# A gated delta recurrence before a mixture of experts: values carried in spare rows of the state

## The chip, the cores and the metric

The kernel runs on one core of a Trainium2 chip. The core has a matrix engine (TensorE, here PE, with its weight loads shown apart), a vector engine (VectorE, DVE), a scalar engine (ScalarE, ACT), GpSimd (POOL) and SyncE (SP), which here does nothing but issue transfers (DMA). Each engine works through its own instructions in order and waits on semaphores. The metric is the time of one execution on the device in microseconds (us); the figure for a kernel is the median of its runs.

## The reference

Two blocks follow each other, all in float32.

The first is a delta-rule recurrence over 4 batches, 8 heads, 768 steps and a head width of 48. Per batch and head a 48x48 state starts at zero:

```
k_n = k / (norm(k) + 1e-6)
for t in range(768):
    y[t]  = q[t] @ state
    v_old = k_n[t] @ state
    state = state + beta[t] * outer(k_n[t], v[t] - v_old)
```

The result, turned to 3072 tokens of width 384, goes into a mixture of experts with 4 groups of 4 experts. Each token takes the best group by `x @ w_group`, then the best expert of that group, and its output is the product of the two softmax weights with `relu(x @ w1) @ w2`, with w1 of 384x1024 and w2 of 1024x384.

## The kernel before

**The recurrence by chunks.** The 768 steps are cut into 24 chunks of 32 (`C`, `NCH`). All four batches lie side by side in the 128 partitions (32 steps each), and the 8 heads are handled as 4 pairs. Inside a chunk the recurrence is a triangular system, which is inverted explicitly. Four chunks (`RG`) form a group, and one call of `inverse(g)` makes the inverses for the whole group on DVE, in some 120 small instructions (L276 to L374). ACT then spreads the result into `mtb` (L385). `inverse` also yields the norms of the keys, `norm[g]`.

**Work per chunk.** `advance(u)` (L407) has four stages, separated by `yield`:

1. `a_ps` holds the norm-scaled values plus key times state. The scaled values `vh` come from `scale(u)` on DVE (L400), and they get into `a_ps` by a product with the identity (L413); 16 small products with the state follow (L419). ACT copies `a_ps`, negated, to `f` (L423). Query times state goes to `o_ps` (L428).
2. `w_ps` is the inverse times `f` (L436), copied to `w` (L439).
3. `s_ps` adds keys times `w` to the state, which lives in PSUM (L446). Two ACT instructions copy it to `s_bd` in SBUF (L452).
4. The masked query-key products `gq` times `w` complete `o_ps` (L460 in the first 14 chunks, L465 in the last ten), and ACT copies it to `x` (L469).

`s_bd` holds, per pair of heads, 48 rows of one head at partitions 0 to 47 and 48 rows of the other at 64 to 111, so that partitions 48 to 63 and 112 to 127 are empty. The keys and queries `kqt` are laid out in the same way, with zeros in these rows.

`gram(u)` makes the products of keys with keys and queries; it runs ten chunks ahead (`LEAD`). `mask(u)` (L261) multiplies `gq` on DVE by a 0/1 mask. It writes each 32-wide product twice, once per parity of the batch, which stage 4 needs where two batches share one product (L460). In the last ten chunks L465 uses one half only.

**What sets the order.** The whole section is scheduled by hand: every engine runs its instructions in the order in which Python emits them. The loop at L693 emits chunk u. The DVE work of `inverse` and of the routing is a set of generators; `work(n)` lets each of them issue instructions up to a share of a time budget, so the budgets of a chunk, `work(10)`, `work(9)`, `work(14)`, `work(12)`, decide where DVE's instructions stand between the rest. At the end of chunk u come `mask(u + 1)`, `scale(u + 2)` and then SP's transfers: `load_kq(u + 12)` (512 KB, L192, up to u = 11), `load_kv(u + 3)` (448 KB, L196; three buffers, `NV`), the store of `x` (L753), and in some chunks a piece of the first expert's weights (L150, L156). `scale(u)` reads the value half of `kv`, stage 3 the key half. Before the loop, `bursts` ties the first loads to ACT instructions between the first grams, and the first group is inverted, after which `mask(0)`, `scale(1)` and `mtb` follow.

`idle_products` (L686) issues products whose result nobody reads, on PE, behind the last chunk and during the sorting of tokens.

**The experts.** Tokens are sorted by expert, gathered, and each of the 16 experts runs on PE: `hidden` (L872), then `second` (L891), which makes the output in three column blocks of 128 and calls `between(j)` after each. For the last expert `turn_out` (L918) turns the three blocks of each of the two token tiles back by PE, multiplies all 384 columns by the gate on DVE (L925), and scatters the rows by an indirect transfer from POOL (L909).

## Time and profile before

| | |
|---|---|
| median of 3 runs | 523.79 us (521.79 to 524.82) |
| profiled execution | 517.99 us, span 516.0 us, granted clock 0.992 |
| PE busy | 472.9 us (92%) |
| DVE busy | 251.0 us (49%) |
| ACT busy | 185.9 us (36%) |
| POOL busy | 194.1 us (38%) |
| identity product, L413 | 48 instructions, 23.4 us busy |
| state products, L419 / L428 | 20.5 / 19.4 us busy |
| state copy on ACT, L452 | 46 instructions, 37.0 us busy |
| mask, L265 / scaling, L400 | 16.1 / 13.7 us busy on DVE |
| loads of k and v, L196 | 24 of 448 KB, 3.8 us from issue to landing (median) |

PE shows two instructions for each float32 product. The recurrence takes the first 244 us or so of the span, the experts the rest. A share of busy time is an average over both: DVE's 49% is nearly full in the first and mostly idle in the second. In a row of the timeline the first number is the start from the beginning of the span, the second the time taken; a bracket tells how long the engine was idle before and what ended it.

### The profile page before, as it was taken

What the parts mean: (1) busy time and instruction counts of PE and PEld (TensorE: products, weight loads), DVE (VectorE), ACT (ScalarE), POOL (GpSimd) and SP (SyncE); (2) the same over time, 40 slices, a digit from 0 to 9 for tenths busy, and PEclk for the clock granted to TensorE, in tenths of its full rate; (3) what the DMA queues carried; (4) which work ended last, traced back from release to release, by engine and by line L of the source; (5) the groups of instructions that cost most, each with busy time, mean ns of one, the idle gap of its engine ahead of it and who ended that gap; (6) DMA issues with size and microseconds to landing.
All of it is one profiled execution on the core that took longest, in us unless ns stands there. A gap on an engine that the chain in (4) does not pass through costs nothing.

```text
span 516.0 us, 18196 instructions
## 1 busy us (share of the span) xinstructions
PE 472.9 (92%) x7832; PEld 437.1 (85%) x7832; DVE 251.0 (49%) x830; ACT 185.9 (36%) x389; POOL 194.1 (38%) x288
## 2 busy tenths in 40 slices
PE   3446999999999999997999999999999999999993
PEld 3335778888888888884999999999999999999992
DVE  2999999999999995435420122012201111011110
ACT  3224767677676776740111211121111111111110
POOL 0040200623707344001264644565536544454312
PEclk9999999999999999999899999999999999999998
DMA  5681444444323545210887786687879878879651
GB/s 175 237 296 47 149 144 155 169 147 151 132 71 125 172 152 164 71 34 27 230 289 231 235 288 217 212 293 262 248 224 312 294 244 276 269 271 306 214 170 43
DMA packets 57331, 99.94 MB, mean 194 GB/s; under 512 B 18973, under 2 KB 41431, under 8 KB 57249
## 3 DMA queue, kind: packets, MB, share of 16 engines
q1 hardware_dynamic: 51329, 88.76, 51.9%
q0 software_dynamic: 5920, 10.00, 6.1%
q8 instruction: 63, 1.03, 0.8%
q14 instruction: 19, 0.16, 0.1%
HBM read 84.61 MB, written 14.27 MB: 192 GB/s over the span
## 4 chain that ended last, share of the span: by engine, by line
PE 57%; DMA 20%; DVE 7%; SPq 5%; ACT 4%; issue 4%; POOL 2%; DVEq 0%; POOLq 0%; ACTq 0%
PE h_ps L878 12%; PE y_ps L897 12%; DMA y_dram<-yq 9%; PE w_ps L436 5%; DMA out_dram<-yo,to_i 5%; PE s_ps L446 5%; DMA yr<-y_dram 4%; SPq L937 4%; PE a_ps L419 3%; PE l_ps L494 3%; ACT s_bd L452 3%; PE o_ps L460 3%; PE o_ps L428 3%; PE g_ps L248 2%; PE a_ps L413 2%
## 5 line engine op out<-in xcount | busy, mean ns | idle before, releaser
L878 PE MATMUL h_ps<-xt,w 128*128 128x224 f32 (+15 forms) x768 | 133.8, 334 | 0.6 <-DVE xt L844 0.6
L897 PE MATMUL y_ps<-hid,w 128*128 128x224 f32 (+15 forms) x768 | 132.2, 331 | 0.0
L878 PEld LDWEIGHTS h_ps<-xt,w 128*128 128x128 f32 x768 | 130.5, 192 | 1.3 <-DVE xt L844 0.7
L897 PEld LDWEIGHTS y_ps<-hid,w 128*128 128x128 f32 x768 | 129.0, 190 | 0.3
L850 POOL DMA_INDIRECT xq<-x_dram,from_q x92 | 87.6, 952 | 34.7 <-issue 24.2
L881 ACT ACTIVATE hid<-h_ps 128x448 f32<-128x448 f32 (+15 forms) x64 | 32.1, 501 | 111.8 <-PE h_ps L878 98.3
L900 DVE COPY yt<-y_ps 128x232 f32<-128x232 f32 (+13 forms) x14 | 5.1, 365 | 135.0 <-PE y_ps L897 135.0
L909 POOL DMA_INDIRECT out_dram<-yo,to_i x32 | 34.1, 1065 | 95.6 <-DVE yo L947 85.4
L902 ACT ACTIVATE yt<-y_ps 128x224 f32<-128x224 f32 (+15 forms) x34 | 11.4, 336 | 116.6 <-PE y_ps L897 116.6
L363 DVE TENSOR_TENSOR m<-m,t 128x81 f32<-128x81 f32 (+13 forms) x156 | 51.8, 332 | 0.0
L357 DVE TENSOR_TENSOR t<-m 128x81 f32<-128x81 f32 (+13 forms) x156 | 51.5, 330 | 0.2
L452 ACT ACTIVATE s_bd<-s_ps 48x768 f32<-48x768 f32 x46 | 37.0, 804 | 13.3 <-PE s_ps L446 12.7
L340 DVE SCALAR_TENSOR_TENSOR m<-m 128x29 f32<-128x29 f32 (+27 forms) x174 | 40.1, 234 | 0.4
L947 DVE TENSOR_SCALAR yo<-yr,gate 128x384 f32<-128x384 f32 (+14 forms) x28 | 11.2, 415 | 54.4 <-DMA yr<-y_dram 45.2
L385 ACT ACTIVATE mtb<-mt,con 128x256 f32<-128x256 f32 x47 | 34.3, 744 | 0.6 <-DVE mt L374 0.5
L248 PE MATMUL g_ps<-kqt 48*32 48x64 f32 (+1 forms) x1216 | 18.5, 241 | 14.6 <-issue 10.0
L436 PE MATMUL w_ps<-f,mtb 64*64 64x48 f32 x768 | 28.0, 224 | 2.9 <-DVE mtb L383 2.9
L436 PEld LDWEIGHTS w_ps<-f,mtb 64*64 64x64 f32 x768 | 25.1, 138 | 5.1 <-ACT mtb L385 3.1
L419 PEld LDWEIGHTS a_ps<-s_bd,kqt 128*32 128x32 f32 x736 | 15.5, 112 | 15.5 <-ACT s_bd L452 7.3
L248 PEld LDWEIGHTS g_ps<-kqt 48*32 48x32 f32 x1216 | 14.7, 118 | 16.4 <-issue 10.7
L533 POOL TENSOR_TENSOR acc<-acc,hots 128x16 f32<-128x16 f32 x16 | 5.7, 354 | 60.1 <-DVE hots L531 59.1
L446 PE MATMUL s_ps<-w,kv 32*128 32x96 f32 x736 | 27.3, 286 | 0.0
(147 smaller groups left out, 581.0 us busy)
## 6 DMA issues: line engine op xcount, KB each, us to landing
w<-in_w_dram SPq DMA_DIRECT2D x29, 1536.0 KB, 12.2
kv<-in_kv_dram SPq DMA_DIRECT2D x24, 448.0 KB, 3.8
kqt<-in_kq_dram SPq DMA_DIRECT2D x20, 512.0 KB, 4.0
x_dram<-x SPq DMA_DIRECT2D x24, 192.0 KB, 2.5
w<-in_w_dram SPq DMA_DIRECT2D x24, 128.0 KB, 3.2
y_dram<-yq SPq DMA_DIRECT2D x36, 84.0 KB, 8.8
yr<-y_dram SPq DMA_DIRECT2D x14, 192.0 KB, 2.4
kqt<-in_kq_dram SPq DMA_DIRECT2D x8, 256.0 KB, 4.1
```

What stands on the lines that cost most here:

```text
L248: nc.tensor.matmul(g_out[quads[b], hh * NP + j, of], lhsT=kqt[rows, 0, j, quads[b]], rhs=kqt[rows, of, j, quads[b]], start=True, stop=True ...
L340: nc.vector.scalar_tensor_tensor(row, in0=m[:, j, 0:j], scalar=m[:, i, j:j + 1], in1=row, op0=ALU.mult, op1=ALU.add)
L357: nc.vector.tensor_tensor(tv, m[:, j + 2:, j:j + 1].to_broadcast([128, n, j]), m[:, j:j + 1, 0:j].to_broadcast([128, n, j]), op=ALU.mult)
L363: nc.vector.tensor_tensor(below, below, tv, op=ALU.add)
L385: nc.scalar.activation(mtb[:, rows, a], from_, ACT.Copy, scale=by)
L436: nc.tensor.matmul(w_ps[b, h], lhsT=mt[b, uu * H + (h % 2) * NP + h // 2], rhs=f[b, h], start=True, stop=True, skip_group_check=True)
L446: nc.tensor.matmul(s_at[:, b, j], lhsT=k[quads[b], j], rhs=w[quads[b], 2 * j:2 * j + 2], start=(u == 0 and j == 0), stop=True, skip_group_ ...
L452: nc.scalar.activation(s_bd[rows, :, :, hh, :], s_at[rows, :, :, hh * D:(hh + 1) * D], ACT.Copy)
L850: nc.gpsimd.indirect_dma_start(out=xq[:, g, :], out_offset=None, in_=x_dram[:, :].rearrange("n (q c) -> (n q) c", q=4), in_offset=bass.Ind ...
L878: nc.tensor.matmul(h_ps[:, k], lhsT=w1[:, j, (f + k) * 128:(f + k + 1) * 128], rhs=xt[:, j, 0:R], start=(j == 0), stop=(j == DC - 1), skip ...
L897: nc.tensor.matmul(y_ps, lhsT=w2[:, f, j * 128:(j + 1) * 128], rhs=hid[:, f], start=(f == 0), stop=(f == FC - 1))
L909: put = nc.gpsimd.indirect_dma_start(out=out[:, :], out_offset=bass.IndirectOffsetOnAxis(ap=to[0:P, i:i + 1], axis=0), in_=yo[0:P, :], in_ ...
```

## The change

**Values through the state product.** The host writes ones into the empty rows of the keys, so that row 48 + r of each half selects step r (or 16 + r) of the chunk. `scale(u)` still makes `vh` on DVE, and then SP issues eight transfers, one per batch and half, each 16 rows of 384 values (24 KB), from `vh` into the empty rows of `s_bd`. The 16 products of keys with the state then add the scaled values by themselves, and the identity product is removed; chunk 0, which had only the identity product, now has the 16 products. `s_bd` becomes two buffers used in turn, both cleared at the start.

**Order.** `scale(u + 2)` moves from the end of chunk u to a place inside what was `work(14)`, and the eight transfers stand there in SP's order, ahead of the loads and the store of the chunk. In the first loads, the first `kv` and two `kq` go ahead of the second `kv` and the last part of the constants.

**Masks.** For the last ten chunks `mask` writes one 32-wide product instead of two, with a mask of its own among the constants.

**Idle products.** Three are added before the first inverse is applied; those during the sorting go from 4 to 5.5, and all use another operand than the identity.

**The last expert.** Its output blocks are turned as they come, block by block for both token tiles (`turn_last`), into two PSUM tiles per token tile. DVE multiplies the first two blocks at once after the second is turned, then the third, and then the rows are scattered.

```diff
+        s_bds = [ap_.tile([128, B, NP, 2, D], F32, name=f"s_bd{i}") for i in range(2)]
...
-            2 * RG: [(kv_[0], [lambda: load_kv(0), lambda: load_con(2), lambda: load_kv(1)])],
-            2 * RG + 2: [of_kq(2 * RG), of_kq(2 * RG + 1),
+            2 * RG: [(kv_[0], [lambda: load_kv(0)]), of_kq(2 * RG), of_kq(2 * RG + 1)],
+            2 * RG + 2: [(kv_[1], [lambda: load_kv(1), lambda: load_con(2)]),
                          (kv_[2], [lambda: load_kv(2),
...
         def mask(u):
+            if u + LEAD >= NCH:
+                gqs[u] = gqm.rearrange("p h a t -> p (h a t)")[:, 0:H * C].rearrange(
+                    "p (h t) -> p h t", t=C)
+                nc.vector.tensor_tensor(gqs[u], raws.pop(u), cut["causal"][:, None, :].to_broadcast(
+                    [128, H, C]), op=ALU.mult)
+                return
...
         def scale(u):
-            vhs[u] = vh
+            for b in range(B):
+                for half in range(2):
+                    row = b * C + half * C // 2
+                    nc.sync.dma_start(out=s_bds[u % 2][half * 64 + D:half * 64 + 64, b].rearrange(
+                        "p j f d -> p (j f d)"),
+                        in_=vh[row:row + C // 2].rearrange("p h d -> p (h d)"))
+            scaled.add(u)
...
         def advance(u):
-            nc.tensor.matmul(a_ps.rearrange("p h d -> p (h d)"), lhsT=ident,
-                             rhs=vh.rearrange("p h d -> p (h d)"), start=True, stop=(u == 0),
-                             skip_group_check=True)
-            if u > 0:
-                for j in range(NP):
-                    for b in range(B):
-                        nc.tensor.matmul(a_ps[quads[b], 2 * j:2 * j + 2, :],
-                                         lhsT=kqt[:, 0, j, quads[b]], rhs=s_bd[:, b, j],
-                                         start=False, stop=True, skip_group_check=True)
+            for j in range(NP):
+                for b in range(B):
+                    nc.tensor.matmul(a_ps[quads[b], 2 * j:2 * j + 2, :],
+                                     lhsT=kqt[:, 0, j, quads[b]], rhs=s_bd[:, b, j],
+                                     start=(j == 0), stop=True, skip_group_check=True)
...
-                    nc.scalar.activation(s_bd[rows, :, :, hh, :],
+                    nc.scalar.activation(s_bds[(u + 1) % 2][rows, :, :, hh, :],
...
                 work(4)
+                if 0 in turned_over and 0 in css:
+                    idle_products(*[H * D] * 3, rhs=css.pop(0))
...
-                work(14)
+                work(5)
+                if u + 2 < NCH:
+                    scale(u + 2)
+                work(9)
...
                     mask(u + 1)
-                if u + 2 < NCH:
-                    scale(u + 2)
...
-            idle_products(*[H * D] * 4)
+            idle_products(*[H * D] * 5, H * D // 2)
...
+    def turn_last(yt, Ps, to, by):
+        tiles = [(ps.tile([P, 2, 4, BL], F32, tag="o", name="o_ps"),
+                  ps.tile([P, 1, 4, BL], F32, tag="h", name="o_ps", bufs=3),
+                  mp.tile([128, DM], F32, tag="yo", name="yo", bufs=4)) for P in Ps]
+        def turn(j):
+            for i, P in enumerate(Ps):
+                nc.tensor.transpose(
+                    out=tiles[i][j // 2][:, j % 2].rearrange("p q c -> p (q c)"),
+                    in_=yt[:, j, i * TILE:i * TILE + P], identity=ident)
+        def weigh(part):
+            for i, P in enumerate(Ps):
+                ks = slice(0, 2) if part == 0 else slice(2, 3)
+                yo = tiles[i][2]
+                nc.vector.tensor_scalar(
+                    yo[0:P].rearrange("p (q k c) -> p k q c", q=4, k=DC)[:, ks],
+                    tiles[i][part], by[0:P, i:i + 1], None, op0=ALU.mult)
+                if part:
+                    scatter(yo, P, to, i)
+        return turn, weigh
...
             def late(n):
+                if e == NE - 1 and n > 0:
+                    if n == 1:
+                        last_out.extend(turn_last(yts[e], tiles_of[e], to_i[:, e], gate[:, e]))
+                    last_out[0](n - 1)
+                    if n == 2:
+                        last_out[1](0)
...
-        for i in range(T):
-            turn_out(yts[NE - 1], tiles_of[NE - 1][i], to_i[:, NE - 1], gate[:, NE - 1], i)
+        last_out[0](2)
+        last_out[1](1)
...
+    for half in range(2):
+        r = np.arange(64 - D)
+        kq[:, half, D + r, 0, :, :, half * (64 - D) + r] = 1.0
```

## The prediction

> **What bounds the kernel now.** I read the page's slices first (which engine is full where), then the table of windows cut at the chunks of the recurrence, then the timeline of one chunk, and last SyncE's queue (SP) with the landing times of its transfers. First the two slice lines and three lines of the table of windows (stretch, length, then busy us of PE, its weight loads, DVE, ACT, POOL, and granted clock, DMA share, GB/s):
>
> ```profile
> PE   3446999999999999997999999999999999999993
> DVE  2999999999999995435420122012201111011110
> ...
> 84.17:91.71 7.54, 7.54 (x236) 6.36 (x235) 7.50 (x33) 5.71 (x11) 1.22 (x4) 1.00 0.48 161
> 178.30:185.40 7.10, 6.96 (x207) 5.90 (x207) 7.07 (x31) 5.02 (x10) 0.98 (x2) 1.00 0.53 160
> 200.30:207.40 7.10, 6.96 (x207) 5.90 (x207) 2.29 (x12) 4.99 (x9) 1.99 (x3) 1.00 0.57 176
> ```
>
> From 44 to 193 us two engines are full together: PE, and DVE with about 2 us of idle time in all. After 193 DVE is free. A cut on PE alone therefore buys little before 193, and every DVE wait there is paid, after the slack between the two. That slack shows in the last rows: DVE ends chunk u's work 2 to 5 us after PE began chunk u+1 (scaling at 102.77, PE's chunk began at 98.97), and PE needs its mask about 6 us in. So DVE can slip 2 to 4 us unseen.
>
> From the timeline: matmuls of the old product around one chunk border (start, length), the first and last rows that date the sum below, and DVE's scalings.
>
> ```profile
> 42.55 0.55 DVE L400 TENSOR_TENSOR vh<-kv,normt 128x384 f32<-128x384 f32 x1
> 82.26 1.14 PE L460 MATMUL o_ps<-w,gqm 64*64 64x48 f32 x32
> 83.33 0.91 PE L413 MATMUL a_ps<-vh,con 128*128 128x384 f32 x2
> 84.17 0.87 PE L419 MATMUL a_ps<-s_bd,kqt 128*32 128x96 f32 x32
> ...
> 102.77 0.54 DVE L400 TENSOR_TENSOR vh<-kv,normt 128x384 f32<-128x384 f32 x1
> 111.53 0.54 DVE L400 TENSOR_TENSOR vh<-kv,normt 128x384 f32<-128x384 f32 x1
> ...
> 223.51 0.87 PE L419 MATMUL a_ps<-s_bd,kqt 128*32 128x96 f32 x32 [0.16 <-ACT s_bd L452]
> ```
>
> From SP's queue and its source lines: four issues in a row, the next one, a chunk's usual three issues, and the landing of the k/v loads.
>
> ```profile
> 18.33 1.75 SPq L192 DMA_DIRECT2D kqt<-in_kq_dram  x4
> 20.18 0.38 SPq L202 DMA_DIRECT2D con<-in_const_dram  x1
> ...
> 85.75 0.33 SPq L192 DMA_DIRECT2D kqt<-in_kq_dram  x1
> 89.16 0.33 SPq L196 DMA_DIRECT2D kv<-in_kv_dram  x1
> 91.50 0.33 SPq L753 DMA_DIRECT2D x_dram<-x  x1
> ...
> L196 SPq DMA_DIRECT2D kv<-in_kv_dram x24: 327/328/423, 23.1 to 205.7; - x24
> DMA to landing us min/median/max: 3.0/3.8/5.8
> ```
>
> An issue alone takes 0.33 us; in a row they start every (20.18 - 18.33) / 4 = 0.46 us. A k/v load lands 3.8 us after its issue. SP is idle most of a chunk, so today none of this is seen.
>
> **The change, part by part.**
>
> The identity product (L413) goes: 0.84 us from its start to L419's (83.33 to 84.17), 23 times. In chunks 1 to 13 it is on PE's path: 0.84 x 13 = 11 us. From chunk 14 PE already waits for ACT's copy of the state (L452, idle 0.16), so it is worth nothing there. But before 193 us DVE is as full as PE. What can really be had is DVE's 2 us of idle time plus what DVE itself loses: the half masks, 0.67 us to about 0.35 (128x256 rows of DVE take 0.35 to 0.43), seven of ten of them before 193, so 2 us. Gain at best 4 us, if nothing new appears.
>
> Something new does appear, on SP. Today chunk u ends with mask(u+1), scale(u+2), and then SP issues kq(u+12), kv(u+3), x(u), none of which waits for the scaling. Afterwards scale(u+2) stands before DVE's last 9 + 12 units, and is followed by eight transfers of 24 KB into the spare rows. In the compiled order SP's row is: eight issues that wait for vh(u+2), then kq(u+12), kv(u+3), x(u). And scale(u+3), in the next chunk, reads kv(u+3). That closes a ring: scaling s, eight issues, the loads behind them, scaling s+1. No buffer opens it, since kv has three. One turn, with the k/q load (s = 2 to 13):
> - scaling 0.55, hand-over to SP 0.05;
> - eight issues x 0.46 = 3.7. Bounds 0.38 (0.33 plus the gap of 0.05) and 0.67 (near 172 us, four issues of L150, one of them 1.03, take 2.5 in all), so 3.0 to 5.4; I take 0.46, the unhindered row;
> - kq's issue 0.46;
> - kv's landing. Bounds: 3.0, the shortest, and 5.8, the longest. The 512 KB of k/q are just ahead of it, so I take 4.2, between the median 3.8 and 4.5, the value at 169 us, just behind the loads of L150;
> - back to DVE 0.05.
> Sum 9.0 us. From s = 14 there is no k/q load: 0.55 + 0.05 + 3.7 + 3.65 + 0.05 = 8.0.
>
> Against this stands DVE's own time from one scaling to the next. I laid the durations of today's DVE rows along the changed order: 8.7, 10.6, 9.1, then 6.2, 7.3, 8.5, 9.3 repeating, up to s = 14; then 7.3, 8.2, 9.1, 6.0, 7.0, 7.0, 3.7, 0.8, 4.6. Each step takes the longer of the two. Twelve steps at 9.0 or more: 9.0 x 8 + 9.1 + 10.6 + 9.3 x 2 = 110.3. Nine at 8.0 or more: 8.0 x 7 + 8.2 + 9.1 = 73.3. Scaling 1 is at 42.55 today and stays there (DVE's chain before it is unchanged), scaling 2 follows 5.9 later by the same rows, 48.4. So scaling 23 starts at 48.4 + 110.3 + 73.3 = 232.0. Its eight transfers need 0.6 + 3.3 to the last issue and 2.3 to land (x, L753, lands in 1.9 to 2.6), so chunk 23's first state product starts at 238.2. Today it starts at 223.51: **14.7 us later**. DVE waits in most chunks, PE behind it, and the 0.84 us become idle time.
>
> The Trainium skill, "DMA: Bandwidth & Descriptors", section "Rules for kernel authors", speaks against such transfers: many small ones should be coalesced, and under 64 KB one pays mostly overhead. Its section "Anatomy of one DMA" gives 2.0 us + bytes / 436e3 (fitted on the GpSimd path); by that estimate the loads land after 4.25 us (both, from kq's issue) and 3.05 (kv alone), the turns are 8.6 and 7.4, and the sum is 7.5 us later instead of 14.7. The row (3.8 for kv) is slower than the rule, and the row decides.
>
> Other parts. First state product for chunk 0: 16 small matmuls that wait for the first eight transfers (issued after the burst, at 33 us; landed near 39), then the two grams and three idle products behind them; w_ps today starts at 43.59 and would start at 45 to 47. It then runs warm: the same w_ps group takes 1.95 us at 43.59 and 1.14 later, so chunk 0 is about 4 us shorter, and PE is at chunk 1 no later than now. DVE does not wait for PE there: 0. The second memset of the state (1.34 us) lies in DVE's idle 8.5 us before the first transpose: 0; its cover gone, it would cost 1.3 once. Reordered first loads and 16 KB more of constants: 0: the load for scaling 0, issued at 23.08, is in by 28.9 even at the longest landing, and scaling 0 runs at 30.7. Extra idle products before the experts: 1.5 x 0.7 = 1.05 us inside PE's idle 2.04 us at 240.5. They may keep the clock up: the first expert's 48 products take 11.03 us, while 9.40 x 224/232 = 9.1 would be its share; between 0 and -2, I take -1. Last expert by thirds: two transposes now stand before the last 16 products (+0.25), and DVE multiplies 2/3 and 1/3 in four pieces (estimate 2 x 0.44 + 0.3 to the first scatter, today 0.6 from 507.27); between -0.4 and +0.5, I take +0.3.
>
> Sum: +14.7 - 1 + 0.3 = +14. The profiled execution (span 516.0, 517.99 in all) is 5.8 us below the median of the runs; I put the difference on the median: 523.8 + 14 = 538.
>
> **The rivals.**
> 1. The ring is short enough to hide, and it is faster. For: issues were never seen with 16 rows, and kv can land in 3.2. It needs turns under about 7.3 and 6.5, so that only the 6.2 steps wait a little. Then the 4 us above and the -1 remain: 519. Against: that takes nearly every bound at its lowest; issues at 0.38 and a landing at 3.2, with k/q just ahead delaying nothing, make 7.3 and 6.9. If k/q delays it by 0.4 (7.7 and 6.9), the sum is 0, near 523. 0.13 for faster, 0.07 for no change.
> 2. Part hidden: turns of 8.0 to 8.6 (kv at its median or faster behind k/q) make +3 to +8 by the same sum, near 530. 0.15.
> 3. PE's clock falls in the new gaps. For: w_ps takes 1.95 at 43.59, after 3 us of idle time, at a granted clock shown as 1.00. PE would have about 2 us of gap per chunk; half a chunk cold costs 1.7, which the gap mostly covers up to s = 13, and about 0.8 x 9 = 7 after: 545. 0.14. The Trainium skill, "TensorE: Matmul & The Clock Gate", section "Why this matters for your kernels", puts the danger at idle gaps over about 3 us; by it the gaps here would cost nothing.
> 4. Issues stall as near 172 us, one in four for 0.6 to 1.1 more: turns 9.9 and 8.9, +31, 554. 0.09.
>
> **How the numbers follow.** The forecast case, the ring with turns near 9.0 and 8.0, has 0.42, and its own range is +8 to +23 (turns 8.6 to 9.5): 531 to 547. The range for 8 in 10 reaches from the case of no change, a little below (521), to 552: it leaves out most of rival 1 and all of rival 4. 0.5% is 2.6 us, what a measurement of this kernel can tell from no change. Faster 0.13, same 0.07, slower 0.15 + 0.42 + 0.14 + 0.09 = 0.80.
>
> **What the profile after would show.** If right: DVE's idle time before the scaling, 1 to 3 us in every chunk whose DVE work is short, ended by the k/v load; eight SP issues every 0.46 us, then kq and kv; scalings about 9.0 and 8.0 us apart; PE idle about 2 us per chunk, from 52 on; the experts unchanged in length. If wrong: scalings at today's distances with SP quiet, or PE waiting where DVE does not, for the spare rows themselves. What would make it wrong: issues of 16 rows much cheaper than 0.33 us, or loads that land before their turn.

## Result and profile after

The changed kernel takes 598.67 us (median of four runs, 593.87 to 599.99), the kernel before 522.79 in the same comparison: a ratio of 1.145, with a 95% interval of 1.135 to 1.156. It is slower by some 76 us. (Ratios, here and below, leave out executions in a slower state, over 1.5% above the fastest of the same kernel; medians take in all.) The prediction was slower too, by the mechanism that came true, but at 538 us: a fifth of the loss. The profiled execution took 599.45 us, with a span of 597.4 against 516.0 before.

From the page of the kernel after, the slices of PE and DVE and the granted clock, and two groups (busy time, mean of one, then the idle time of the engine just before them and what ended most of it):

```profile
PE   4339888688979868887999999999999999999993
DVE  4979776665775785722325211111111111111110
...
PEclk9999877886687797678777999999999999999998
...
L432 PE MATMUL a_ps<-s_bd,kqt 128*32 128x96 f32 x768 | 46.8, 320 | 38.8 <-DMA s_bd<-vh 29.5
...
L411 DVE TENSOR_TENSOR vh<-kv,normt 128x384 f32<-128x384 f32 x24 | 13.4, 558 | 85.0 <-DMA kv<-in_kv_dram 33.9
```

In the recurrence neither DVE nor PE is full any more: mostly 6 to 8 tenths where there were 9. DVE sits idle for 85.0 us ahead of the scaling (L411). The engine's busy time is what it was (249.4 us against 251.0), so nothing was added to it; it waits. The timeline of one turn of the ring, first DVE's scalings, then SP's queue (start, length):

```profile
50.70 0.56 DVE L411 TENSOR_TENSOR vh<-kv,normt 128x384 f32<-128x384 f32 x1
...
158.40 0.56 DVE L411 TENSOR_TENSOR vh<-kv,normt 128x384 f32<-128x384 f32 x1 [4.04 <-DMA kv<-in_kv_dram]
...
170.24 0.56 DVE L411 TENSOR_TENSOR vh<-kv,normt 128x384 f32<-128x384 f32 x1 [3.40 <-issue]
...
159.02 5.60 SPq L419 DMA_DIRECT2D s_bd<-vh  x8
164.67 0.58 SPq L194 DMA_DIRECT2D kqt<-in_kq_dram  x1
165.35 0.38 SPq L198 DMA_DIRECT2D kv<-in_kv_dram  x1
```

The turn reads straight off: scaling at 158.40, first issue 159.02, eight issues until 164.67, k/q load, k/v load issued at 165.35, next scaling at 170.24. That is 0.62 + 5.65 + 0.68 + 4.89 = 11.84 us. The profile puts only 33.9 of the 85.0 us down to the k/v load, 33.2 to the x store, which no scaling reads, and 17.9 to "issue". That all of it is the k/v load is read from the distance: in the 21 turns the next scaling follows the load's issue after 3.9 to 6.0 us (median 4.6), whatever the wait is put down to. The first two experiments test it.

Scaling 2 starts at 50.70 and scaling 23 at 290.06, 239.4 us for 21 turns; before it was 52.5 to 214.9, 162.4 us. These 77.0 us are the loss, nearly whole. Chunk 23's first state product starts 8.3 us behind scaling 23, at 298.36 (before 223.51, so +74.9). From there to the first expert's first product it takes 5.8 us longer, and the experts to the end of the span 0.7 (272.6 against 271.9): together 81.4, the difference of the spans. The 5.8 us are in two rows of the windows, the first of after, the second of before (stretch, length, busy PE, weight loads, DVE, ACT, POOL, granted clock, DMA share, GB/s):

```profile
298.36:324.79 26.43, 24.95 (x241) 19.84 (x241) 8.24 (x42) 3.85 (x11) 2.16 (x2) 0.68 0.10 29
```

```profile
223.51:244.15 20.64, 16.25 (x236) 12.73 (x236) 8.39 (x42) 3.85 (x11) 2.15 (x2) 1.00 0.12 37
```

The same work of the other engines, five more PE instructions, and a granted clock of 0.68 instead of 1.00. The added idle products are not the reason: in the run of the rest alone (below), which has them too, the same stretch takes 20.7 us.

### The profile page after: what moved, and what is told of

The parts are those of the page before. It is cut to its first block, busy times and chain, and to the rows that moved or that the text cites. A ratio compares the mean times of both kernels' runs of the same rounds, so it can differ in the third digit from the quotient of the medians.

```text
span 597.4 us, 18637 instructions
## 1 busy us (share of the span) xinstructions
PE 515.6 (86%) x7826; PEld 478.4 (80%) x7826; DVE 249.4 (42%) x833; ACT 186.4 (31%) x390; POOL 187.7 (31%) x288
## 3 DMA queue, kind: packets, MB, share of 16 engines
q1 hardware_dynamic: 57473, 93.50, 49.6%
## 4 chain that ended last, share of the span: by engine, by line
PE 60%; DMA 15%; issue 7%; DVE 6%; SPq 6%; POOL 3%; ACT 2%; POOLq 0%; DVEq 0%; ACTq 0%
PE y_ps L913 16%; PE h_ps L894 16%; DMA out_dram<-yo,to_i 6%; DMA s_bd<-vh 5%; SPq L419 5%; PE a_ps L432 4%; PE w_ps L449 4%; PE o_ps L441 4%; PE s_ps L459 3%; PE l_ps L507 2%; PE i_ps L668 2%; POOL xq L866 2%; PE t_ps L499 2%; DMA x_dram<-x 2%; PE s_ps L615 2%
## 5 line engine op out<-in xcount | busy, mean ns | idle before, releaser
L894 PE MATMUL h_ps<-xt,w 128*128 128x224 f32 (+15 forms) x768 | 132.1, 331 | 0.8 <-DVE xt L860 0.8
L894 PEld LDWEIGHTS h_ps<-xt,w 128*128 128x128 f32 x768 | 129.1, 190 | 1.2 <-DVE xt L860 0.9
L432 PE MATMUL a_ps<-s_bd,kqt 128*32 128x96 f32 x768 | 46.8, 320 | 38.8 <-DMA s_bd<-vh 29.5
L432 PEld LDWEIGHTS a_ps<-s_bd,kqt 128*32 128x32 f32 x768 | 31.6, 141 | 49.4 <-issue 21.5
L367 DVE TENSOR_TENSOR t<-m 128x81 f32<-128x81 f32 (+13 forms) x156 | 52.5, 337 | 0.2
L411 DVE TENSOR_TENSOR vh<-kv,normt 128x384 f32<-128x384 f32 x24 | 13.4, 558 | 85.0 <-DMA kv<-in_kv_dram 33.9
L441 PE MATMUL o_ps<-s_bd,kqt 128*32 128x96 f32 x736 | 33.5, 322 | 0.7 <-ACT x L482 0.7
L459 PE MATMUL s_ps<-w,kv 32*128 32x96 f32 x736 | 30.0, 300 | 2.1 <-issue 1.3
L436 ACT ACTIVATE f<-a_ps 128x384 f32<-128x384 f32 x24 | 11.8, 491 | 63.9 <-PE a_ps L432 63.9
L449 PE MATMUL w_ps<-f,mtb 64*64 64x48 f32 x768 | 31.0, 237 | 0.0
```

Of the source, the lines that this page charges most:

```text
L367: nc.vector.tensor_tensor(tv, m[:, j + 2:, j:j + 1].to_broadcast([128, n, j]), m[:, j:j + 1, 0:j].to_broadcast([128, n, j]), op=ALU.mult)
L432: nc.tensor.matmul(a_ps[quads[b], 2 * j:2 * j + 2, :], lhsT=kqt[:, 0, j, quads[b]], rhs=s_bd[:, b, j], start=(j == 0), stop=True, skip_gro ...
L441: nc.tensor.matmul(o_ps[quads[b], 2 * j:2 * j + 2, :], lhsT=kqt[:, 1, j, quads[b]], rhs=s_bd[:, b, j], start=(j == 0), stop=False, skip_gr ...
L449: nc.tensor.matmul(w_ps[b, h], lhsT=mt[b, uu * H + (h % 2) * NP + h // 2], rhs=f[b, h], start=True, stop=True, skip_group_check=True)
L459: nc.tensor.matmul(s_at[:, b, j], lhsT=k[quads[b], j], rhs=w[quads[b], 2 * j:2 * j + 2], start=(u == 0 and j == 0), stop=True, skip_group_ ...
L894: nc.tensor.matmul(h_ps[:, k], lhsT=w1[:, j, (f + k) * 128:(f + k + 1) * 128], rhs=xt[:, j, 0:R], start=(j == 0), stop=(j == DC - 1), skip ...
```

## The experiments

All paces in one table first. "21 turns" is the time from scaling 2 to scaling 23, from DVE's timeline in each profile; ratios are those of the times to the kernel before in the same comparison. In three kernels only the attention may be read, as said below; the last row is read by its time alone.

| kernel | scaling 2 | scaling 23 | 21 turns | time, us | ratio (95%) |
|---|---|---|---|---|---|
| before | 52.5 | 214.9 | 162.4 | 522.79 | 1 |
| changed | 50.7 | 290.1 | 239.4 | 598.67 | 1.145 (1.135 to 1.156) |
| loads first | 50.5 | 236.5 | 186.0 | 540.84 | 1.042 (1.038 to 1.046) |
| four k/v buffers | 50.1 | 241.6 | 191.5 | 545.38 | 1.047 (1.042 to 1.053) |
| rest alone | 52.0 | 215.7 | 163.7 | 516.94 | 0.997 (0.994 to 0.999) |
| rest, no early idle products | 52.0 | 214.5 | 162.6 | 516.87 | 1.000 (0.997 to 1.003) |
| sixteen transfers | 50.8 | 402.8 | 352.0 | 717.2 | 1.384 (1.378 to 1.390) |
| narrow transfers | 49.5 | 286.3 | 236.8 | attention only | |
| idle products in the gaps | 49.2 | 288.5 | 239.4 | attention only | |
| ring, filled | 49.3 | 286.4 | 237.0 | 591.02 | 1.137 (1.128 to 1.147) |
| loads first, half | 50.8 | 219.9 | 169.1 | attention only | |
| loads first, via DRAM | 49.6 | 235.0 | 185.4 | 541.97 | 1.042 (1.031 to 1.054) |
| loads on ScalarE's queue | 52.1 | 252.1 | 200.0 | 554.75 | 1.062 (1.052 to 1.071) |
| no SP waits | 50.1 | 231.7 | 181.6 | 537.46 | 1.036 (1.029 to 1.043) |
| and first loads of before | 47.4 | 226.6 | 179.2 | 534.01 | 1.036 (1.029 to 1.044) |
| and filled | 47.2 | 227.1 | 179.9 | 536.17 | 1.032 (1.026 to 1.039) |
| via DRAM, late | 47.8 | 236.2 | 188.4 | 540.78 | 1.037 (1.032 to 1.042) |
| via DRAM, late, filled | | | | 541.11 | 1.032 (1.023 to 1.041) |

### Is it the ring? Loads first, and a fourth buffer

```diff
+                if u + NB < NCH:
+                    load_kq(u + NB)
+                if u + NV < NCH:
+                    load_kv(u + NV)
                 if u + 2 < NCH:
                     scale(u + 2)
                 work(9)
```

(and the same lines gone from the end of the chunk.)

> The changed kernel with one move: in each turn SP issues the k/q load of chunk u+12 and the k/v load of chunk u+3 ahead of the scaling of chunk u+2 and its eight transfers, not behind them. Nothing is computed differently. Theory A (ring on SP: scaling, eight issues, k/v load, next scaling; 11.9 us a turn with and 10.8 us without the k/q load): the k/v load is then issued at least 5.6 us sooner, VectorE's idle time ahead of the scaling (85.0 us in all) falls under 25 us, the scalings come 8 to 9 us apart, the time is 520 to 540 us. Theory B (the eight transfers land too late for TensorE, which waits for them): they are issued up to 1.2 us later than now, so nothing is gained: 595 to 605 us. Theory C (the granted clock, 0.5 to 0.8 in most chunks, bounds TensorE, whatever VectorE does): 580 to 600 us, clock in the chunks as now.

Measured: 540.84 us. The same ring can be opened without a change of SP's order:

```diff
-        NB, NV = LEAD + 2, 3
+        NB, NV = LEAD + 2, 4
...
-                         (kv_[2], [lambda: load_kv(2),
+                         (kv_[2], [lambda: load_kv(2), lambda: load_kv(3),
```

> The changed kernel with four k/v buffers instead of three, the fourth loaded at the start; SP's order stays. Theory A: the k/v load behind scaling u+2's transfers is then for the scaling two turns on, so that a ring of 11.9 or 10.8 us spans two turns (6.0 or 5.4 us each), under VectorE's own 8.0 us: waits ahead of the scaling under 25 us, 520 to 540 us. Theory B: transfers of the spare rows unchanged, 590 to 605 us. Theory C: 580 to 600 us.

Measured: 545.38 us. The waits of DVE from 40 to 250 us (who, for what; us in total, times, longest), of loads first and then of four buffers:

```profile
DVE vh L411 <- DMA s_bd<-vh: 17.2, 5, 7.0
...
DVE vh L411 <- DMA kv<-in_kv_dram: 1.5, 1, 1.5
```

```profile
DVE vh L411 <- DMA x_dram<-x: 9.9, 3, 7.8
```

By two different means the wait for the k/v load is gone or nearly so, and 53 to 58 us with it, so the ring is shown to be the mechanism (A). The waits that the first kernel keeps are for the transfers themselves: `vh` has two buffers, so a scaling waits until the transfers of the scaling before the last have read theirs. B falls: the first of the two issues the transfers behind the loads, later in the turn than the changed kernel, and it is the faster. Both kernels stay at A's upper bound or above it, 4 to 5% over the kernel before, and that remainder is taken up below.

### Issues or bytes? Sixteen transfers, and narrow ones

```diff
             for b in range(B):
                 for half in range(2):
-                    row = b * C + half * C // 2
+                    for q in range(2):
+                        row = b * C + half * C // 2 + q * C // 4
+                        to = half * 64 + D + q * C // 4
...
-                        in_=vh[row:row + C // 2].rearrange("p h d -> p (h d)"))
+                            in_=vh[row:row + C // 4].rearrange("p h d -> p (h d)"))
```

> The changed kernel with sixteen transfers of 8 rows (12 KB) a chunk instead of eight of 16 rows (24 KB); the same bytes, order unchanged. Theory A with issues as the price: eight more issues of 0.46 to 0.70 us in each of 21 turns, +77 to +118 us: 675 to 717 us. Theory A with the bytes as the price of the turn (the issues stall because the queue moves 192 KB a chunk): 600 to 620 us. Theory B: the last transfer lands later by the same issues, but the two chunks of lead hide it: 600 to 640 us.

Measured: 717.2 us, and 352.0 us for the 21 turns: 5.36 us more a turn for eight more issues, 0.67 us each. SP's queue of this kernel:

```profile
141.78 11.24 SPq L421 DMA_DIRECT2D s_bd<-vh  x16
153.07 0.44 SPq L194 DMA_DIRECT2D kqt<-in_kq_dram  x1
153.61 0.38 SPq L198 DMA_DIRECT2D kv<-in_kv_dram  x1
...
158.66 10.87 SPq L421 DMA_DIRECT2D s_bd<-vh  x16
```

The opposite cut keeps eight issues and takes seven eighths of the bytes away:

```diff
-                        "p j f d -> p (j f d)"),
-                        in_=vh[row:row + C // 2].rearrange("p h d -> p (h d)"))
+                        "p j f d -> p (j f d)")[:, 0:D],
+                        in_=vh[row:row + C // 2].rearrange("p h d -> p (h d)")[:, 0:D])
```

> The changed kernel, SP's order as in it, with the eight transfers cut to 48 of 384 columns (3 KB each in place of 24 KB): seven heads' scaled values in eight are left out. It parts the price of an issue from that of its bytes; the attention alone is read (first to last w_ps, 253.5 us in the changed kernel, 11.0 a chunk), since wrong scores may change how many tokens each expert gets. If an issue costs its 0.58 to 0.70 us whatever it moves, and the k/v load lands as now: 240 to 255 us. If the 196 KB ahead of the k/v load in the queues is what makes it land late (4.8 us in place of 3.8) and what stalls one issue in eight for 0.5 to 1.2 us: turns shorter by 1.5 to 2.5 us, 200 to 222 us.

Measured in the attention alone, since most of the scaled values are missing: 251.0 us from the first to the last w_ps (253.5 in the changed kernel), 236.8 for the 21 turns (239.4). The line of the transfers and one of the k/v load's landing, from the views by source line (duration in ns min/median/max), and the eight issues of one turn:

```profile
L419 SPq DMA_DIRECT2D s_bd<-vh x192: 507/580/1837, 31.3 to 292.2; - x192
...
DMA to landing us min/median/max: 3.7/4.4/6.0
...
157.40 5.94 SPq L419 DMA_DIRECT2D s_bd<-vh  x8
```

With 3 KB instead of 24 KB an issue has the same median, 0.58 us, the same longest ones (1.84 against 1.82), and the turn is as long to 0.1 us. The k/v load, with an eighth of the bytes ahead of it, lands after 4.4 us (median), where in the changed kernel the next scaling follows its issue after 4.6. So the price is the issue, not what it moves.

### The rest of the change, alone

```diff
-            for b in range(B):
-                for half in range(2):
-                    row = b * C + half * C // 2
-                    nc.sync.dma_start(out=s_bds[u % 2][...], in_=vh[...])
-            scaled.add(u)
+            vhs[u] = vh
```

(and with it the identity product, one state buffer, the place of `scale` and the first loads as before.)

> The kernel before with all of the change but the spare rows: half-width masks in the last chunks, the idle products' new operands and number, the last expert by thirds; scaled values go to a_ps through the identity product as before. If the whole loss is the spare rows' (A, B and C alike): half masks -2 to 0 us, idle products -1 to 0 us, last expert -0.5 to +0.5 us, so 520 to 524 us against 523. If some other part costs (the clock falling at the end of attention, where the stretch from the last a_ps to the first expert took 26.4 us against 20.6): up to 529 us.

Measured: 516.94 us where the kernel before took 518.29, a ratio of 0.997. The early idle products hold the first w_ps there (44.54 us against 43.59), so they were taken out as well:

```diff
-                if 0 in turned_over and 0 in css:
-                    idle_products(*[H * D] * 3, rhs=css.pop(0))
```

> The kernel before with the half-width masks, the 5.5 idle products at the sorting and the last expert by thirds, without the three idle products ahead of the first w_ps, which held it by 1 us in the run of the rest alone (w_ps from 44.54 against 43.59 us). If that 1 us reaches the end: 514 to 517 us where the rest alone is 516.9. If the first chunks' TensorE is then cold as before and VectorE sets the pace anyway: 516 to 518 us.

Measured: 516.87 us, a ratio of 1.000 (0.997 to 1.003). The first w_ps starts at 43.01 us; the 1.5 us that it gains do not reach the end by anything that these runs can tell. So the loss belongs to the spare rows and what came with them, the place of the scaling and the order of the first loads. The rest alone is the one version whose interval lies under 1, by 0.1 to 0.6%; without the early idle products the interval holds 1.

### Has the clock a part in the ring?

```diff
             xs[u] = x
+            if 0 < u < NCH - 1:
+                for _ in range(8):
+                    nc.tensor.matmul(s_ps[:, 3, 384:512], lhsT=ident, rhs=ident, start=True,
+                                     stop=True, skip_group_check=True)
```

> The changed kernel (SP's order as in it) with eight idle products of 128 columns on TensorE behind the last product of each chunk from 1 to 22, in unused PSUM columns: 2.4 us at full clock, in the gap that each turn leaves. Theory A (ring): the granted clock rises in the chunks, to 0.9 or more, but the turns stay at 10.8 to 11.9 us: 590 to 605 us. Theory C (the low clock is what makes the turns long): with the clock up the time falls to 530 to 570 us.

These products disturb the sums of the state that share their PSUM bank, so the experts get other numbers of tokens and only the attention is read: 239.4 us for the 21 turns, as without them. Two rows of the windows of this kernel and two of the changed kernel, the columns as above:

```profile
50.00:100.00 50.00, 44.02 (x1219) 39.11 (x1219) 35.93 (x129) 29.62 (x56) 4.04 (x14) 0.96 0.37 114
100.00:150.00 50.00, 44.15 (x1047) 40.78 (x1047) 32.76 (x117) 24.43 (x49) 11.61 (x30) 0.87 0.37 114
```

```profile
50.00:100.00 50.00, 40.89 (x1073) 35.16 (x1067) 36.10 (x129) 28.87 (x55) 4.04 (x14) 0.83 0.38 115
100.00:150.00 50.00, 40.58 (x1024) 35.35 (x1020) 33.64 (x122) 24.00 (x48) 12.42 (x30) 0.77 0.38 114
```

The clock rises from 0.83 and 0.77 to 0.96 and 0.87, and the turns do not get shorter. In a second form, which disturbs nothing, an idle product takes the place of the removed identity product:

```diff
             a_ps = ps.tile([128, H, D], F32, tag="s", name=f"a_ps{u}")
+            if u > 0:
+                nc.tensor.matmul(a_ps.rearrange("p h d -> p (h d)"), lhsT=ident,
+                                 rhs=cut["below"][:, 0:H * D], start=True, stop=True,
+                                 skip_group_check=True)
```

> The changed kernel, SP's order and ring as in it, with the same idle product ahead of each a_ps. Theory A (the ring sets the turns): 239 us from scaling 2 to 23 as now, 590 to 603 us. Theory C (the clock): 530 to 570 us.

Measured: 591.02 us and 237.0 us for the 21 turns, at a mean granted clock of 0.943 against 0.895 over the span. Theory C falls for the ring: the turns keep their length, to 0.1 us each, whatever the clock. The profiled span is 10.2 us shorter (587.2 against 597.4): scaling 23 comes 3.7 us earlier than in the changed kernel, the other 6.5 lie behind it.

### What is left when the ring is open: SP itself

The remainder was first tested with less work for SP, in the kernel with the loads first.

```diff
-            for b in range(B):
+            for b in range(B // 2):
                 for half in range(2):
```

> The loads-first kernel (540.8 us) with four of the eight transfers a chunk: those of batches 2 and 3 are left out, so their scaled values are missing from the result. Theory A2, what is left of the loss there is SP's own time: its k/q load, k/v load, eight transfers and x store fill 8.4 to 9.2 us of a turn of 9 us with few pauses, against VectorE's 8.0; with four transfers SP needs some 5 to 6 us, VectorE is the bound again: 515 to 524 us. Theory D, the rest is TensorE's: sixteen more products ahead of each f, and waits of a_ps for the copied state (9.4 us in ten waits), whatever SP does: 534 to 541 us.

Measured in the attention alone (the time holds experts with other numbers of tokens): 169.1 us for the 21 turns, and 182.4 us from the first w_ps to the last, against 182.2 before. Four transfers a chunk, placed behind the loads, cost almost nothing. What eight cost without SP's waits was tested next (the loads and the store gone from the end of the chunk):

```diff
-        NB, NV = LEAD + 2, 3
+        NB, NV = LEAD + 2, 4
...
+                if u and u + NB - 1 < NCH:
+                    load_kq(u + NB - 1)
+                if u + NV - 1 < NCH:
+                    load_kv(u + NV - 1)
                 if u + 2 < NCH:
                     scale(u + 2)
+                if u:
+                    nc.sync.dma_start(out=x_dram[(u - 1) * 128:u * 128], in_=done.pop(u - 1))
```

> The changed kernel, nothing left out and all eight transfers on SP, with SP's own waits taken away besides the ring: a fourth k/v buffer, so that the k/v load of u+3 needs chunk u-1's buffer; the k/q load of u+11 in place of u+12; both ahead of the transfers of u+2; the x store of chunk u-1 behind them. Theory A2 in the form: SP is the bound of the loads-first kernel because its issues (6.8 to 7.4 us a chunk) and its waits for TensorE's state products and for x add up to 8.8 us. Without the waits the first to the last w_ps takes 182 to 188 us (before 182.2, loads first 202.7), and the time is 519 to 527 us. If the issues alone are over 8 us a chunk (stalls of 1.2 to 2.0 us in one of eight): 190 to 200 us there, 527 to 538 us. Theory D (TensorE): 202 us, 538 to 542 us.

Measured: 537.46 us, 197.3 us from the first to the last w_ps. That is the second of the three cases, in which the issues alone are too many. The same kernel with the first loads of before,

```diff
-            2 * RG: [(kv_[0], [lambda: load_kv(0)]), of_kq(2 * RG), of_kq(2 * RG + 1)],
-            2 * RG + 2: [(kv_[1], [lambda: load_kv(1), lambda: load_con(2)]),
+            2 * RG: [(kv_[0], [lambda: load_kv(0), lambda: load_con(2), lambda: load_kv(1)])],
+            2 * RG + 2: [of_kq(2 * RG), of_kq(2 * RG + 1),
```

> The kernel without SP's waits, with the first loads in the order of before as well (the third part of the constants behind the first k/v load, not behind the second). In the changed kernel GpSimd's copies of the constants started at 34.66 us instead of 28.60 and VectorE waited 3.08 us for the roots (42.14 instead of 39.78). If it is the order of the loads: that wait is gone and all that follows is 2 to 3 us earlier, 517 to 525 us. If the transfers of scaling 0 are what is late there: no difference from the run without SP's waits.

Measured: 534.01 us; the ratios of the two are equal within their intervals, so the time does not tell them apart. The traces do. DVE's and POOL's timeline where they meet, of the run without this edit:

```profile
41.58 0.35 DVE L327 RECIPROCAL r<-nrm 128x32 f32<-128x32 f32 x1 [3.69 <-POOL nrm L302]
```

and with it:

```profile
38.87 0.35 DVE L327 RECIPROCAL r<-nrm 128x32 f32<-128x32 f32 x1
...
28.52 0.34 POOL L686 COPY what<-con 128x48 f32<-128x48 f32 x1 [27.65 <-DMA con<-in_const_dram]
```

In the changed kernel that copy on POOL starts at 34.66, since the third part of the constants is issued at 29.08 (before: 23.46). The roots come behind it in POOL's order, and DVE waits for them. The scalings 1 and 2 are 2.7 us earlier with the edit. Then the idle product was put ahead of each a_ps in this kernel too:

> The kernel without SP's waits and with the first loads of before (eight direct transfers a chunk, 534.0 us, 179.2 us from scaling 2 to 23), with the same idle product ahead of each a_ps. Theory E: 165 to 172 us from scaling 2 to 23, 518 to 527 us. Theory A2 (SP's issues, 8 us or more a chunk with their stalls, set the pace whatever the clock): 177 to 182 us, 530 to 537 us. Theory F: as A2, with the clock falling in the same number of stretches.

Measured: 536.17 us, 179.9 us for the 21 turns as against 179.2 without it. SP's queue of this kernel:

```profile
118.67 5.53 SPq L419 DMA_DIRECT2D s_bd<-vh  x8
124.62 0.33 SPq L761 DMA_DIRECT2D x_dram<-x  x1
125.01 0.50 SPq L194 DMA_DIRECT2D kqt<-in_kq_dram  x1
125.62 1.86 SPq L198 DMA_DIRECT2D kv<-in_kv_dram  x1
127.58 5.94 SPq L419 DMA_DIRECT2D s_bd<-vh  x8
133.61 1.38 SPq L761 DMA_DIRECT2D x_dram<-x  x1
135.04 0.43 SPq L194 DMA_DIRECT2D kqt<-in_kq_dram  x1
135.56 0.40 SPq L198 DMA_DIRECT2D kv<-in_kv_dram  x1
136.07 6.12 SPq L419 DMA_DIRECT2D s_bd<-vh  x8
```

There is hardly a pause in it: one turn takes 8.91 us, the next 8.49, of eleven issues that wait for next to nothing, among them single ones of 1.38 and 1.86. The turns of 21 take 8.57 us on average (179.9 / 21), with a granted clock of 0.96 to 1.00 in each of five stretches from 47 to 227 us. Over the whole stretch SP pauses eight times for more than 0.15 us, 9.1 us in all, so its issues alone fill some 171 us where the kernel before needs 162.4. DVE's wait for them is in its own list, where they hold the two buffers of `vh`:

```profile
DVE vh L411 <- DMA s_bd<-vh: 16.7, 5, 7.5
```

That is nearly the 17.5 us by which the 21 turns are longer than before. So with eight direct transfers SP's own queue has become the bound (A2), at 8.6 us where DVE's chunk takes 7.7. No run gave `vh` a third buffer.

### Three transfers through DRAM

```diff
-            for b in range(B):
-                ...
+            vd = yp.tile([128, DM], F32, tag="vd", name=f"vd{u}")
+            nc.sync.dma_start(out=vd, in_=vh.rearrange("p h d -> p (h d)"))
+            for half in range(2):
+                nc.sync.dma_start(
+                    out=s_bds[u % 2][half * 64 + D:half * 64 + 64].rearrange("p b j f d -> p b (j f d)"),
+                    in_=vd.rearrange("(b f r) e -> f r b e", b=B, f=2)[half])
```

> The loads-first kernel with nothing left out, the scaled values moved in three transfers a chunk: one of 192 KB to DRAM, and, once that has landed, two of 96 KB from there into the spare rows. Theory A2: SP issues 3 + 3 a chunk, 3 us, and waits some 3 to 4 us for the landing in DRAM, 6 to 7 us of a turn of 8: 516 to 526 us. If the wait for the landing holds the x store and the next loads long enough to make SP the bound again: 530 to 545 us. Theory D: 534 to 541 us.

Measured: 541.97 us, in the second case. From SP's waits:

```profile
SPq L419 <- DMA vd<-vh: 89.6, 21, 6.6
SPq L198 <- PE s_ps L459: 17.5, 10, 4.7
```

It waits 4.3 us a chunk for the landing. What the issues saved, this wait took. So in the next kernel the two transfers back are issued one turn later, on top of the edits for SP's waits and the first loads:

```diff
+            if u < 2:
+                spare_rows()
+            else:
+                moved.append(spare_rows)
...
+                if moved:
+                    moved.pop(0)()
                 if u + 2 < NCH:
                     scale(u + 2)
```

> The kernel without SP's waits and with the first loads of before, nothing left out, the scaled values moved in three transfers a chunk through DRAM, where the two back from DRAM are issued one turn later, when the first has long landed; so SP neither issues eight times nor waits for a landing (4.3 us a chunk in the run via DRAM). Theory A2 (SP's queue, issues and waits together, is all that is left of the loss): SP needs some 3 us a chunk, VectorE sets the pace as before, scaling 2 to scaling 23 takes 162 to 168 us (before 162.4, loads first 186.0), 514 to 522 us. Theory D (the new form of the product costs TensorE or its waits something of its own): scalings as far apart as without SP's waits (179 to 182 us), 530 to 538 us.

Measured: 540.78 us. SP now waits for DVE, 73.5 us in 19 waits, DVE's waits ahead of the scaling are 1.1 us in all, and yet the 21 turns take 188.4 us. Part of the time is the way through DRAM itself: chunk 0 waits 11.2 us for its rows (8.0 with eight direct transfers), and the first w_ps starts at 50.88 instead of 46.42. But from the first to the last w_ps, too, it is 196.9 us, against 192.4 with eight direct transfers and 182.2 before. With SP idle the pace is no better, so something else bounds this kernel. PE's timeline in the longest step (14.2 us from one w_ps to the next), and two rows of the windows:

```profile
101.76 1.13 PE L457 MATMUL w_ps<-f,mtb 64*64 64x48 f32 x32
102.83 0.43 PE L251 MATMUL g_ps<-kqt 48*32 48x64 f32 x25
106.30 0.89 PE L251 MATMUL g_ps<-kqt 48*32 48x64 f32 x39 [3.05 <-issue]
...
111.41 1.95 PE L481 MATMUL o_ps<-w,gqm 64*64 64x48 f32 x32
...
119.69 1.14 PE L481 MATMUL o_ps<-w,gqm 64*64 64x48 f32 x32
...
99.83:113.28 13.45, 10.40 (x239) 9.32 (x237) 11.17 (x33) 6.24 (x14) 7.24 (x19) 0.68 0.68 203
113.28:120.80 7.52, 7.52 (x236) 6.83 (x234) 6.53 (x29) 4.45 (x9) 4.22 (x8) 0.89 0.12 38
```

PE is full and warm, pauses for 3.05 us in the middle of a group (for nothing that this view shows), and the same groups then take 1.95 instead of 1.14 us until about 115. The chunk takes 13.45 us where the next takes 7.52: 3.05 of pause and 2.9 more of busy time.

The trace tells more of these pauses. In the run via DRAM the largest one stands ahead of the same product, the 39th from the end of its group; and the page of both lists a DMA queue of its own kind:

```profile
100.92 0.89 PE L251 MATMUL g_ps<-kqt 48*32 48x64 f32 x39 [3.29 <-issue]
...
q8 instruction: 63, 1.03, 0.9%
```

That is 63 transfers of 16 KB. In the late kernel PE's five pauses of over 0.5 us that are put down to "issue" between 50 and 230 us fall on its products number 1747, 2383, 2892, 3401 and 3909, each distance a multiple of 127 to within one, and PE goes on 1.3 to 1.5 us after one of these transfers has ended. In the other kernels such pauses stand at such steps too. With its weight load a product is two instructions, and 63 x 254 is 16002 where PE ran 15652 of them. So the pauses look like waits for PE's own instructions. No run tested that, and why a few of them come late is open. The five sum to 7.8 us; the clock, 0.84, 0.86, 0.96 and 0.87 in four stretches of 40 us from 47 us on, costs at most 40 x (0.16 + 0.14 + 0.04 + 0.13) = 19 us by an estimate from these figures. Together that is about the 26.0 us by which the 21 turns are longer than before.

The idle product was the test of whether a fuller PE avoids it:

> The kernel via DRAM with the late transfers, and an idle product of the size of the removed identity product (identity times 384 constant columns, 0.9 us) at its old place ahead of each a_ps from chunk 1, overwritten by the products that follow; nothing waits for new data. There SP has slack, VectorE no longer waits for the scaling (1.1 us in all), and still scaling 2 to 23 took 188 us against 162.4, with the granted clock between 0.50 and 0.81 in the stretches of 66 to 90, 106 to 114 and 186 to 202 us, where groups of products take 1.95 instead of 1.14 us. Theory E (opened, the rest is TensorE's clock, which falls in the gaps that the removed product leaves): clock over 0.97 in the chunks, 162 to 170 us from scaling 2 to 23, 516 to 525 us. Theory F (the gaps come from waits and pauses that a filler doesn't remove): 530 to 545 us, clock as without it.

Measured: 541.11 us, a ratio of 1.032 (1.023 to 1.041), not to be told from 1.037 without it. A filler does not cure it (F): in its profile, too, PE pauses for 2.03 and 2.34 us at such steps. That a lowered clock follows for some 8 us is seen in the trace, but no run took the pauses alone away.

### The loads on ScalarE's queue

```diff
-            nc.sync.dma_start(out=kqt_[u % NB][:, half],
+            (nc.scalar if u >= NB else nc.sync).dma_start(out=kqt_[u % NB][:, half],
...
-            nc.sync.dma_start(out=kv_[u % NV], in_=kv_d[u])
+            (nc.scalar if u >= NV else nc.sync).dma_start(out=kv_[u % NV], in_=kv_d[u])
```

> The loads-first kernel, nothing left out, with the k/q and k/v loads of the running chunks issued from ScalarE's queue, so that SP has the eight transfers and the x store alone, some 6.2 us a chunk. Theory A2: SP has room, ScalarE loses 0.8 to 1 us a chunk of its idle time: 516 to 528 us. If ScalarE's issues stand on the way from a_ps to f or from the state to its copy, or its wait for the state's products holds the mask factors: 528 to 545 us. Theory D: 534 to 541 us.

Measured: 554.75 us, outside of all three cases, worse than with the loads on SP. ScalarE's timeline shows where a part of it goes, with PE's last products that read the buffer of the k/v load:

```profile
117.71 1.15 PE L459 MATMUL s_ps<-w,kv 32*128 32x96 f32 x32
...
122.65 0.33 ACTq L194 DMA_DIRECT2D kqt<-in_kq_dram  x1
125.39 0.33 ACTq L198 DMA_DIRECT2D kv<-in_kv_dram  x1
125.82 0.49 ACT L436 ACTIVATE f<-a_ps 128x384 f32<-128x384 f32 x1 [3.35 <-DMA kqt<-in_kq_dram]
```

The k/v load is issued 2.74 us behind the k/q load, with ScalarE standing behind it, and f, on the recurrence's path, comes 3.35 us later for it. This happens in three turns, 11.2 us in all. What the issue waits for is not shown; the products that read its buffer had ended at 118.86. An issue of 0.33 us is cheap; the wait ahead of it is not.

## Why the prediction was right and wrong

**The mechanism was right.** The ring on SP (scaling, eight issues, k/q and k/v load, next scaling) was named with its members, and both ways of opening it take most of the loss away. That nothing on DVE or PE pays for the removed product was right too: with four transfers a chunk, which cost next to nothing, the way from the first to the last w_ps takes 182.4 us, before 182.2. DVE's own steps were laid out rightly as well: 8.7, 10.6, 9.1, 6.2, 7.3, 8.5 predicted, 8.7, 10.7, 9.0, 6.2, 7.3, 8.4 measured in that run.

**The terms of the turn were mis-sized, and this is the step that failed.** Measured in the turn at 158.40, in the order of the sum: scaling and hand-over 0.62 (predicted 0.60), right. Eight issues 5.65 (3.7): they start every 0.70 us, not every 0.46. The 0.46 came from a row of loads from DRAM, taken as "the unhindered row"; a transfer from SBUF to SBUF has a median of 0.58 us for itself and single ones up to 1.8. k/q issue 0.68 (0.46). k/v landing 4.89 (4.25 with the way back). Sum 11.84 against 9.0. Over the turns: twelve of 11.88 us on average (scaling 2 at 50.70 to scaling 14 at 193.25) where the sum had 9.2, nine of 10.76 (to 290.06) where it had 8.1. That is 32.3 + 23.5 us, and with scaling 2 at 50.7 instead of 48.4 the whole of the 58.1 us by which scaling 23 came later than predicted (290.1 against 232.0). From there to chunk 23's first product it was 8.3 us instead of 6.2; the timeline puts the last wait ahead of that product (1.00 us at 298.36) down to the copied state, not to the transfers.

**The range was drawn tighter than its own bounds.** The upper bounds in the text, 5.4 for the issues and 5.8 for the landing, make turns of 12.3 and 11.85, that is 12 x 12.3 + 9 x 11.85 = 254 us where the sum had 183.6, and a time near 609. The range took neither; it stopped at turns of 9.5. A price that recurs in 21 turns does not average out. Rival 4 had the issues stall, but priced that at 0.9 us a turn, where its own words, one in four of eight for 0.6 to 1.1 more, make 1.2 to 2.2, and put no later landing beside it; the two together came to 2.6 us a turn (1.95 and 0.64), and the k/q issue to 0.2.

**The upper bound of 5.4 for the issues** was itself too low for some turns (up to 6.3 us in the changed kernel), because no row of the trace before showed this kind of transfer.

**Rival 1 and 2** (hidden, or partly) fell. **Rival 3** (the clock falls in the gaps) came true as an effect: a granted clock of 0.77 and 0.83 in the windows above. As a price it was only behind the recurrence, the 5.8 us; in the ring it cost nothing (239.4 and 237.0 us with a warmer clock). The Trainium skill, "TensorE: Matmul & The Clock Gate", section "Why this matters for your kernels", puts the danger at idle gaps over about 3 us; the trace does not agree. In the timeline of the changed kernel a wait of 2.20 us, with 0.77 us of idle time some 2 us ahead of it, is followed at once by o_ps at 1.88 us, where it took 1.13 a turn earlier:

```profile
59.27 1.13 PE L473 MATMUL o_ps<-w,gqm 64*64 64x48 f32 x32
...
65.38 1.15 PE L459 MATMUL s_ps<-w,kv 32*128 32x96 f32 x32 [0.77 <-ACT gt L256]
66.46 0.84 PE L507 MATMUL l_ps<-wr,xt 128*128 128x20 f32 x6
69.50 1.88 PE L473 MATMUL o_ps<-w,gqm 64*64 64x48 f32 x32 [2.20 <-DVE gqm L275]
```

**The first chunk.** w_ps starts at 47.49 (predicted 45 to 47) and runs warm at 1.13 us, as said. "DVE does not wait for PE there" holds, but "reordered first loads: 0" failed: only the k/v load of scaling 0 was looked at, not the constants, which POOL copies ahead of the roots. It cost 2.4 us at that point (scaling 1 at 44.92 instead of 42.55); the two runs that differ in it do not tell whether this reaches the end.

**The small parts.** The half masks take 0.42 us instead of 0.67 (predicted 0.35); by the run of the rest alone this is no gain that reaches the end. The extra idle products were to lie in PE's idle 2.04 us: in the run of the rest alone they do, and the first expert's 48 products take 9.35 us instead of 11.03 (predicted up to -2); there the products behind the first 48 start 0.5 us sooner, though chunk 23 began 1.1 us later. In the changed kernel twelve of the idle products run cold and take 6.59 us instead of 3.80. The last expert by thirds, +0.3 predicted: in the run of the rest alone the last scatter is issued by 509.99 us, 3.8 us behind the last y_ps product, before 3.9. The experts are unchanged in length, as predicted.

**Transfers against the rule.** The Trainium skill, "DMA: Bandwidth & Descriptors", section "Rules for kernel authors", wants small transfers coalesced. The runs agree in the sign: sixteen cost 118 us more than eight. What counted here was the number of issues, 0.58 us each in the issuing queue for 3 KB and 24 KB alike. Three large transfers by way of DRAM were no faster than eight direct ones (541.97 against 540.84 us), since SP waited for the first of them.

## What to carry to other kernels

Before moving work into DMAs, write down the queue that issues them as an engine with its own time per chunk, count every issue on it with a price from the same kind of transfer, and look for a ring: a load that stands behind issues which wait for the engine that the load feeds. Where the price comes from another kind of transfer, and recurs in every turn, carry its upper bound into the range as often as it recurs. And a product taken off an engine that shares the bound with another need not gain anything (here it did not), while the gaps that come with the change can lower the clock.

## What the runs showed of the hardware that was not expected

- An issue on SP from SBUF to SBUF (16 rows) takes 0.51 us at least, 0.58 in the median, and single ones up to 1.8 in the changed kernel; a load from DRAM 0.33 to 0.38 in the median. The issue of 16 rows takes the same for 3 KB and 24 KB; sixteen of 12 KB take 10.9 to 11.2 us in a row, 0.68 to 0.70 each.
- After a pause of 2.20 us in one place and 3.05 in another, groups of products on TensorE took 1.9 instead of 1.14 us, for some 4 to 8 us.
- 192 KB from SBUF to DRAM made SP wait 4.3 us a chunk (89.6 us in 21 waits) before the way back could be issued.
- PE's unexplained pauses stand 127 products or a multiple of that apart, and PE goes on 0.8 to 1.7 us (mostly 1.2 to 1.5) after a 16 KB transfer of the "instruction" queue has ended. In the kernel before there is one of them in the recurrence (0.65 us), in the late one via DRAM five (0.64 to 3.05 us).
